# Gate sums divided out in the addition of delta, five held units, another order of the work

## The chip, the cores and the metric

The kernel runs on one core of a Trainium2 chip. The metric is device time in microseconds of that core, as the median of several runs. Engines in the profile: PE (TensorE, matrix products; PEld is its weight load), DVE (VectorE), ACT (ScalarE), POOL (GpSimd) and SP (SyncE, which here only issues DMAs). ScalarE issues DMAs too; the two issuers have a DMA ring each.

## The reference

```
# q, k, v, alpha: (4, 8, 768, 48) float32; state (48 x 48) for each of 4 x 8 heads
for t in range(768):
    state = alpha[t][:, None] * state + outer(k[t], v[t])
    y[t]  = q[t] @ state
x = y, heads side by side: (3072, 384)
logits = x @ w_gate                     # 8 experts
w = softmax over the 2 largest logits, 0 for the others
out = x + sum over e of w[e] * (x @ A[e]) @ B[e]      # rank 16 each
```

So a gated linear attention with a decay for every position and channel feeds a mixture of eight low-rank adapters.

## The kernel before

The 768 positions of a batch entry are cut into 6 chunks of 128; a chunk with all 8 heads is a *unit*, and there are 24 units, `u` = 0 to 23, of which 0, 6, 12 and 18 begin a batch entry ("batch 0" to "batch 3"). A unit is a tile of 128 positions x 384 columns. Each unit goes through the same steps, each a small function of the kernel:

- `ln` (ScalarE, mostly two units at once), `cum` (TensorE: sums of the logarithms to the chunk's end, in a PSUM bank), `exp` (ScalarE, twice: the decay and its inverse).
- `ka` and `kg` (GpSimd): `k` times one, `q` times the other, in bf16. Some units do both in one instruction of 128x768, those in `SPLIT` in two of 128x384.
- `tr` and `kq` (TensorE transposes, ScalarE copies), `at` (TensorE: the products of q and k, in the PSUM tile `at_t`), `msk` (VectorE: the causal mask, 128x1024, line 300).
- `vb` (GpSimd: `v` in bf16), `kv` (TensorE adds this chunk to the state in PSUM, `S_t`), `st` (VectorE scales the state by the decay, line 306). From unit to unit of a batch entry `st` and `kv` are a recurrence.
- `av` (TensorE: the unit's rows of y, in a bank), `ysb` (ScalarE copies them to `o_t[u]`), `xb` (GpSimd, bf16 copy, for the even units, `CAST`), `xt` and `xs` (TensorE transposes, ScalarE copies; in bf16 for `CAST` units, in float32 for the others).

The adapters work on *groups* of three units (the last two groups have two and one): `z` (TensorE: `x @ A` and the logits in one bank), `gm` (VectorE, the largest logits), `df`, `ge` and `gx` (difference to the largest, which are among the best two, exponential on ScalarE), `wu` (unnormalized weights), `dn` (their sum), `w` (reciprocal of the sum, and the weights times it, lines 416 and 419), `zw` (z times the weights, line 431), `zt` and `zs` (transposes, ScalarE copy). Then for each unit `dl` (TensorE: delta, in a bank, line 448), `o` (VectorE adds it to `o_t[u]`, line 455) and `out` (the store, issued by SyncE). Unit 23 alone is in `HOLD`: its `dl` is accumulated by TensorE onto its `av` bank, which is kept until then, and its `o` is a copy by ScalarE. The last group, which is unit 23, has its own short forms (lines 402 and 427).

PSUM has the tile `at_t` (two banks), the state `S_t`, and five banks `M_t` that `cum`, `tr`, `av`, `xt`, `z`, `zt` and `dl` share; the last number of an entry of the order says which of the five.

The order of everything is written out by hand in `ORDER`, one list for all engines: each engine takes its instructions in the order of the list, semaphores do the rest. `Sx.u.n` and `Ax.u.n` in it are loads issued by SyncE and by ScalarE: alpha (`a`), `q`, `k` and `v` of a batch entry come in one DMA each (48 rows of 48 numbers for each of 128 partitions), into two buffers of each that take turns. SyncE loads alpha and `q`, ScalarE loads `k` and `v`. A load of batch 2 or 3 waits until its buffer is free.

Of the kernel before, what the change touches and what calls it, by code (L numbers as in the profile page):

```python
# [9 lines left out]
ALU = mybir.AluOpType  # L10
# [3 lines left out]
F4 = mybir.dt.float32  # L14
# [4 lines left out]
DM = H * D  # L19
E = 8  # L20
R = 16
P = 128
# [8 lines left out]
GROUPS = [[0, 1, 2], [3, 4, 5], [6, 7, 8], [9, 10, 11], [12, 13, 14], [15, 16, 17], [18, 19, 20], [21, 22],  # L31
          [23]]
LNS = [[0], [1]] + [[u, u + 1] for u in range(2, NU, 2)]
CAST = set(range(0, NU, 2))
HOLD = {23}
SPLIT = {0, 1, 2, 3, 4, 5, 6, 7, 12, 13, 18, 19}
KEEP = dict(lg=2, ex=5, kg=6, kt=4, am=4, sb=3, vb=4, xs=9, xb=3, mx=3, xe=3, wu=3, dn=3, w=3, zw=3, zs=3)
NS = 6
MB = 5
ORDER = """  # L40
Sa.0.6 Aw.3.0 Sq.0.6 Aw.2.0 Sw.0.0 Ak.0.6 Sw.1.0 Sa.6.6 ln.0 Sq.6.6 ln.1 cum.0.0 cum.1.1 ln.4 exp.0 ln.2 exp.1
cum.2.2 Sa.12.6 ka.0 cum.5.3 Av.0.6 cum.3.4 exp.2 ka.1 exp.3 ka.2 kg.0 kg.1 tr.0.0 cum.4.1 kq.0 ka.3 tr.1.2 exp.5
at.0 kg.2 kq.1 msk.0 exp.4 kg.3 tr.2.4 cw.0 at.1 kg.4 msk.1 tr.3.0 Ak.6.6 kq.2 vb.0 kq.3 at.2 vb.1 kv.0 ka.4 av.0.3
st.1 ysb.0 msk.2 kv.1 vb.2 av.1.2 xb.0 tr.4.1 ysb.1 kg.5 st.2 at.3 xt.0.4 msk.3 ln.8 av.2.0 ka.5 Sq.12.6 kv.2 ln.6
st.3 vb.5 tr.5.3 xs.0 vb.4 ysb.2 cum.6.2 kq.4 cum.7.4 vb.3 kq.5 xb.2 at.4 exp.6 kv.3 msk.4 xt.2.0 xt.1.1 exp.7 ka.6
cum.9.3 st.4 cum.8.2 Av.6.6 xs.2 at.5 ln.10 ka.7 kv.4 msk.5 xs.1 Sa.18.6 exp.8 z.0.4 av.3.0 kg.6 exp.9 gm.0 av.4.1
st.5 ysb.3 kg.7 tr.6.2 ge.0 ysb.4 df.0 gx.0 av.5.3 kq.6 wu.0 kg.8 xt.3.0 dn.0 ysb.5 w.0 tr.7.1 xs.3 zw.0 at.6 kq.7
xt.5.2 msk.6 cum.11.3 xb.4 xs.5 zt.0.0 kg.9 xt.4.4 cum.10.1 xs.4 at.7 Ak.12.6 exp.10 tr.8.2 msk.7 z.1.4 zs.0 kq.8
vb.6 tr.9.1 gm.1 vb.7 exp.11 kv.6 at.8 kg.10 df.1 st.7 gx.1 av.6.0 msk.8 ln.12 av.7.2 kv.7 kq.9 cum.12.3 vb.8 st.8
ysb.6 dl.0.1 at.9 kg.11 ge.1 ysb.7 o.0 tr.10.0 ln.14 msk.9 av.8.2 kq.10 dl.2.1 kv.8 ysb.8 vb.9 dl.1.0 o.2 Sq.18.6  # L50
at.10 exp.12 vb.11 wu.1 cum.13.2 st.9 xt.7.1 xb.8 exp.13 dn.1 o.1 kv.9 xb.6 w.1 tr.11.3 Av.12.6 vb.10 xs.7 zw.1
cum.14.0 kq.11 ka.12 xt.8.2 msk.10 xt.6.1 zt.1.4 xs.8 cum.15.3 xs.6 zs.1 av.9.2 ka.13 exp.14 st.10 dl.3.1 z.2.4 o.3
ysb.9 kg.12 at.11 ln.16 gm.2 kv.10 msk.11 dl.4.0 kg.14 exp.15 tr.12.2 xt.9.1 kq.12 df.2 av.10.3 st.11 xs.9 cum.16.2
ge.2 o.4 gx.2 ysb.10 at.12 kg.13 wu.2 exp.16 tr.14.1 msk.12 dl.5.0 xb.10 kq.14 tr.13.3 kg.15 av.11.2 dn.2 o.5 kq.13
cum.17.1 w.2 Ak.18.6 xt.10.0 ysb.11 at.13 zw.2 xs.10 xt.11.3 msk.13 vb.12 tr.15.2 xs.11 vb.13 kv.12 exp.17 z.3.0
kg.16 st.13 at.14 ln.18 gm.3 av.13.4 msk.14 zt.2.3 kq.15 kv.13 cum.18.1 kg.17 zs.2 ysb.13 av.12.2 df.3 ge.3 st.14
at.15 ysb.12 tr.16.3 msk.15 exp.18 dl.7.4 vb.14 gx.3 tr.17.2 kq.16 wu.3 vb.15 o.7 kv.14 ln.20 vb.16 av.14.1 dn.3
st.15 xb.12 at.16 ysb.14 w.3 cum.19.3 vb.17 msk.16 kq.17 av.15.4 xb.14 Av.18.6 out.2 xt.13.1 exp.19 ka.18 out.7
kv.15 zw.3 xt.14.2 xs.13 at.17 st.16 xs.14 ka.19 xt.12.3 ysb.15 msk.17 zt.3.0 dl.6.1 xs.12 cum.20.2 ln.22 z.4.4
kg.18 o.6 zs.3 dl.8.3 exp.20 kv.16 gm.4 kg.19 tr.18.0 o.8 xt.15.1 kq.18 df.4 st.17 out.8 kg.20 dl.9.2 cum.21.3 xs.15  # L60
out.3 o.9 dl.10.0 gx.4 at.18 exp.21 out.5 o.10 tr.19.1 ge.4 msk.18 out.10 cum.22.2 kq.19 kg.21 av.17.0 out.6 exp.22
dl.11.3 av.16.1 wu.4 o.11 at.19 ysb.17 out.0 dn.4 tr.20.2 msk.19 ysb.16 out.9 vb.18 tr.21.3 kq.20 out.11 xb.16 kv.18
out.4 xt.17.0 kq.21 vb.19 w.4 st.19 at.20 out.1 vb.20 xs.17 xt.16.1 zw.4 cum.23.2 kg.22 xs.16 kv.19 msk.20 exp.23
z.5.3 st.20 at.21 kg.23 gm.5 av.18.0 tr.22.4 msk.21 ysb.18 kv.20 kq.22 av.20.1 ge.5 vb.21 df.5 at.22 st.21 gx.5
ysb.20 av.19.2 vb.22 wu.5 msk.22 zt.4.0 xb.18 ysb.19 kv.21 vb.23 tr.23.4 zs.4 dn.5 xb.20 dl.14.1 st.22 xt.19.2 kq.23
w.5 kv.22 xs.19 o.14 at.23 zw.5 xt.18.0 out.14 xt.20.4 msk.23 av.22.2 xs.18 xs.20 dl.12.1 z.6.3 ysb.22 o.12 xb.22
av.21.0 zt.5.4 gm.6 ysb.21 xt.22.2 dl.13.1 st.23 zs.5 xt.21.0 xs.22 df.6 ge.6 o.13 gx.6 dl.15.4 dl.17.2 xs.21 wu.6
o.15 av.23.1 z.7.0 dn.6 o.17 out.15 ysb.23 dl.16.4 out.13 gm.7 xt.23.2 w.6 out.17 df.7 ge.7 zw.6 gx.7 xs.23 wu.7
o.16 z.8.3 zt.6.2 gm.8 dn.7 out.16 zs.6 df.8 w.7 gx.8 out.12 dl.19.4 wu.8 dl.18.2 zw.7 o.18 zt.7.0 o.19 zs.7 dl.20.2
out.18 dl.21.0 w.8 o.20 dl.22.4 out.19 zw.8 out.20 o.21 zt.8.2 o.22 zs.8 out.21 dl.23 out.22 o.23 out.23  # L70
"""


# [6 lines left out]
def _bc(src: bass.AP, rep: int) -> bass.AP:  # L80
    aps = [list(x) for x in src.ap]
    return bass.AP(tensor=src.tensor, offset=src.offset, ap=aps + [[0, rep]])
# [9 lines left out]
def kernel(  # L92
# [11 lines left out]
    nc = tc.nc  # L104
# [11 lines left out]
    o_t = [big.tile([P, DM], F4, name=f"o_t{u}") for u in range(NU)]  # L116
# [21 lines left out]
    def act_copy(*args):  # L138
        recent[:] = [nc.scalar.copy(*args)]  # L139
# [56 lines left out]
    ex = ring("ex", [P, 2, DM + 2 * NP], F4)  # L196
# [7 lines left out]
    xe = ring("xe", [P, 3, E], F4)  # L204
    wut = ring("wu", [P, 3, E], F4)
    dnt = ring("dn", [P, 3], F4)
    wt = ring("w", [P, 3, E], F4)
    zwt = ring("zw", [P, 3, E, R], F2)
    zst = ring("zs", [P, 3 * HP], F4)
    W = consts.tile([P, NF, NZ], F2, name="W")  # L210
# [14 lines left out]
    def bank(s, i):  # L225
        return M_t[slot[s, i]]
# [112 lines left out]
                    start=(c == 0 and h == 0), stop=(h == H - 1 and u not in HOLD), skip_group_check=True)  # L339

    def ysb(u):
        act_copy(o_t[u], bank("av", u)[:, 0:DM])

    def xb(u):
        nc.gpsimd.tensor_copy(out=xbt[u % KEEP["xb"]], in_=o_t[u])  # L345

    def xt(u):
        if u in CAST:
            t, x, idn = bank("xt", u).bitcast(F2), xbt[u % KEEP["xb"]], ident
        else:  # L350
            t, x, idn = bank("xt", u), o_t[u], ident4
        x = x.rearrange("p (f i) -> p i f", i=NF)
        for i in range(NF):
            nc.tensor.transpose(t[:, i * P:(i + 1) * P], x[:, i, :], idn[:, :])  # L354

    def xs(u):
        t, y = bank("xt", u), xst[u % KEEP["xs"]].rearrange("p i t -> p (i t)")
        if u in CAST:
            act_copy(y.bitcast(F4), t[:, 0:DM // 2])
        else:  # L360
            act_copy(y, t[:, 0:DM])
# [5 lines left out]
    def scratch(g, i):  # L367
        n = len(GROUPS[g])
        lo = 3 * NZ + 3 * E * i
        return bank("z", g)[:, lo:lo + n * E].rearrange("p (n e) -> p n e", n=n)  # L370
# [28 lines left out]
    def wu(g):  # L399
        n = len(GROUPS[g])  # L400
        if n == 1:
            nc.vector.scalar_tensor_tensor(
                out=wut[g % KEEP["wu"]][:, 0, :], in0=zv(g)[:, 0, E * R:NZ], scalar=mx[g % KEEP["mx"]][:, 0, 1:2],
                in1=xe[g % KEEP["xe"]][:, 0, :], op0=ALU.is_ge, op1=ALU.mult, accum_out=dnt[g % KEEP["dn"]][:, 0:1])
            return
        nc.vector.tensor_tensor(out=scratch(g, 1), in0=scratch(g, 1),
                                in1=xe[g % KEEP["xe"]][:, 0:n, :], op=ALU.mult)

    def dn(g):
        n = len(GROUPS[g])  # L410
        nc.vector.tensor_reduce(out=dnt[g % KEEP["dn"]][:, 0:n], in_=scratch(g, 1),
                                op=ALU.add, axis=AX.X)

    def w(g):
        n = len(GROUPS[g])
        nc.vector.reciprocal(out=dnt[g % KEEP["dn"]][:, 0:n], in_=dnt[g % KEEP["dn"]][:, 0:n])
        if n == 1:
            return
        nc.vector.tensor_tensor(out=wt[g % KEEP["w"]][:, 0:n, :], in0=scratch(g, 1),
                                in1=_bc(dnt[g % KEEP["dn"]][:, 0:n], E), op=ALU.mult)  # L420

    def zw(g):
        n = len(GROUPS[g])
        zo = zwt[g % KEEP["zw"]][:, 0:n].rearrange("p n e r -> p (n e) r")
        z3 = zv(g)[:, :, 0:E * R].rearrange("p n (e r) -> p n e r", e=E)
        if n == 1:
            nc.vector.scalar_tensor_tensor(
                out=zo, in0=z3[:, 0], scalar=dnt[g % KEEP["dn"]][:, 0:1], in1=_bc(wut[g % KEEP["wu"]][:, 0, :], R),
                op0=ALU.mult, op1=ALU.mult)
        else:  # L430
            nc.vector.tensor_tensor(out=zwt[g % KEEP["zw"]][:, 0:n], in0=z3, in1=_bc(wt[g % KEEP["w"]][:, 0:n, :], R),  # L431
                                    op=ALU.mult)

    def zt(g):
        t = bank("zt", g).bitcast(F2)
# [15 lines left out]
    def o(u):  # L451
        if u in HOLD:
            act_copy(o_t[u], bank("av", u)[:, 0:DM])
        else:
            nc.vector.tensor_tensor(out=o_t[u], in0=bank("dl", u)[:, 0:DM], in1=o_t[u], op=ALU.add)  # L455

    def store(u):
        b, c = _place(u)
# [50 lines left out]
```

## Time and profile before

| | |
|---|---|
| median of 3 runs | 96.92 us (95.02 to 97.39) |
| the profiled execution | 94.6 us; span from first to last instruction 92.6 us; clock 0.971 |
| busy, share of the span | PE 68.6 us (74%), DVE 62.7 (68%), ACT 64.7 (70%), POOL 62.6 (68%) |
| moved | 24.17 MB, mean 261 GB/s: read 19.28 MB, written 4.72 MB |
| chain that ended last | DMA 33%, DVE 26%, ACT 16%, PE 11%, issue 5% |

A share of busy time is a mean over parts of the span with different limits, so it does not tell what a change is worth; for that one looks where each part of the span waits. In the slices of the page each digit is the busy share of a fortieth of the span in tenths. In the table of groups a row gives line, engine, operation, output and input, shapes and count, then the busy time and the mean duration of one in ns, then the idle time ahead of these instructions and what ended it. A timeline row gives start, duration and instruction.

### The profile page before, as it was taken

What the parts mean: (1) busy time and instruction counts of PE and PEld (TensorE: products, weight loads), DVE (VectorE), ACT (ScalarE), POOL (GpSimd) and SP (SyncE); (2) the same over time, 40 slices, a digit from 0 to 9 for tenths busy, and PEclk for the clock granted to TensorE, in tenths of its full rate; (3) what the DMA queues carried; (4) which work ended last, traced back from release to release, by engine and by line L of the source; (5) the groups of instructions that cost most, each with busy time, mean ns of one, the idle gap of its engine ahead of it and who ended that gap; (6) DMA issues with size and microseconds to landing.
All of it is one profiled execution on the core that took longest, in us unless ns stands there. A gap on an engine that the chain in (4) does not pass through costs nothing.

```text
span 92.6 us, 2795 instructions
## 1 busy us (share of the span) xinstructions
PE 68.6 (74%) x1088; PEld 54.0 (58%) x1088; DVE 62.7 (68%) x165; ACT 64.7 (70%) x164; POOL 62.6 (68%) x82
## 2 busy tenths in 40 slices
PE   0003080888899799959999998999999989994520
PEld 0002050756787697846787886887787878861100
DVE  5000000055956768887999999799999999999920
ACT  5004891695299998869999976999999666744120
POOL 6000087999795899997879999978999994200000
PEclk9999999999999999999999999999999999999855
DMA  1999999999999899999979999999996920216682
GB/s 25 282 309 317 315 317 315 303 314 304 317 312 298 233 309 311 281 303 304 302 229 316 311 281 305 307 306 251 289 383 227 342 94 7 85 52 250 258 295 84
DMA packets 29645, 24.17 MB, mean 261 GB/s; under 512 B 1856, under 2 KB 29632, under 8 KB 29632
## 3 DMA queue, kind: packets, MB, share of 16 engines
q1 hardware_dynamic: 16928, 14.35, 50.0%
q10 hardware_dynamic: 12704, 9.65, 36.6%
q8 instruction: 8, 0.13, 0.6%
q14 instruction: 5, 0.04, 0.2%
HBM read 19.28 MB, written 4.72 MB: 259 GB/s over the span
## 4 chain that ended last, share of the span: by engine, by line
DMA 33%; DVE 26%; ACT 16%; PE 11%; issue 5%; SPq 2%; ACTq 2%; POOL 1%; DVEq 0%
DMA a_t<-in_alpha_dram 18%; DMA kq_t<-in_q_dram 14%; DVE am L300 11%; ACT ex L136 5%; DVE o_t L455 5%; DVE sb L306 3%; ACT xs L139 3%; ACT o_t L139 3%; PE at_t L296 2%; PE M_t L283 2%; ACT lg L136 2%; ACT kt L139 2%; DVE zw L431 2%; PE M_t L448 2%; SPq L155 2%
## 5 line engine op out<-in xcount | busy, mean ns | idle before, releaser
L263 POOL TENSOR_TENSOR kgq<-kq_t,ex 128x384 bf16<-128x384 f32 (+1 forms) x36 | 45.0, 1275 | 12.4 <-ACT lg L136 9.8
L300 DVE TENSOR_TENSOR am<-at_t,mask 128x1024 bf16<-128x1024 f32 x24 | 29.3, 1220 | 20.5 <-PE at_t L296 20.4
L136 ACT ACTIVATE ex<-M_t 128x392 f32<-128x392 f32 (+1 forms) x48 | 21.6, 536 | 0.6 <-PE at_t L296 0.6
L283 PE MATMUL M_t<-ident,kgq 128*128 128x128 bf16 x192 | 17.0, 237 | 2.7 <-POOL kgq L263 2.6
L247 PE MATMUL M_t<-lg,suf 128*128 128x384 bf16 x24 | 8.6, 366 | 12.3 <-ACT lg L136 12.3
L139 ACT COPY kt<-M_t 128x512 f32<-128x512 f32 x24 | 14.6, 618 | 4.1 <-PE M_t L283 3.5
L139 ACT COPY o_t<-M_t 128x384 f32<-128x384 f32 x25 | 12.4, 521 | 5.5 <-PE M_t L337 4.7
L136 ACT ACTIVATE lg<-a_t 128x768 bf16<-128x768 f32 (+1 forms) x13 | 10.5, 824 | 8.0 <-DMA a_t<-in_alpha_dram 7.2
L283 PEld LDWEIGHTS <-kgq 128*128 128x128 bf16 x192 | 12.8, 105 | 4.6 <-POOL kgq L263 3.1
L455 DVE TENSOR_TENSOR o_t<-M_t,o_t 128x384 f32<-128x384 f32 x23 | 12.4, 550 | 1.1 <-PE M_t L448 1.1
L306 DVE TENSOR_TENSOR sb<-S_t,ex 128x384 bf16<-128x384 f32 x20 | 11.0, 549 | 1.2 <-PE S_t L320 1.2
L277 POOL CAST vb<-v_t 128x384 bf16<-128x384 f32 x24 | 11.6, 507 | 0.0
L296 PE MATMUL at_t<-kt 48*128 48x128 bf16 x192 | 10.2, 229 | 1.4 <-DVE am L300 1.0
L337 PE MATMUL M_t<-vb,am 128*128 128x48 bf16 x192 | 9.0, 186 | 0.0
L345 POOL CAST xb<-o_t 128x384 bf16<-128x384 f32 x12 | 6.0, 507 | 4.4 <-ACT o_t L139 4.3
L248 PEld LDWEIGHTS <-ident 128*128 128x128 bf16 x24 | 2.4, 101 | 11.2 <-issue 10.9
L296 PEld LDWEIGHTS <-kt 48*128 48x128 bf16 x192 | 6.2, 98 | 4.1 <-issue 1.9
L448 PE MATMUL M_t<-B_all,zs 128*128 128x384 bf16 x24 | 7.5, 334 | 1.0 <-ACT zs L139 0.8
L337 PEld LDWEIGHTS <-am 128*128 128x128 bf16 x192 | 7.3, 99 | 0.3
L354 PE MATMUL M_t<-ident,o_t 128*128 128x128 f32 x36 | 6.9, 302 | 0.2 <-DVE o_t L455 0.2
L320 PE MATMUL S_t<-vb,kgq 128*128 128x96 bf16 x80 | 7.0, 213 | 0.0
L330 PE MATMUL M_t<-sb,kt 128*128 128x96 bf16 x80 | 6.9, 209 | 0.1
(53 smaller groups left out, 101.0 us busy)
## 6 DMA issues: line engine op xcount, KB each, us to landing
out_dram<-o_t SPq DMA_DIRECT2D x24, 192.0 KB, 2.1
B_st<-in_moe_B_dram ACTq DMA_DIRECT2D x1, 192.0 KB, 2.7
W_st<-in_moe_A_dram SPq DMA_DIRECT2D x2, 96.0 KB, 9.4
a_t<-in_alpha_dram SPq DMA_DIRECT2D x4, 0.2 KB, 12.9
kq_t<-in_q_dram SPq DMA_DIRECT2D x4, 0.2 KB, 16.4
kq_t<-in_k_dram ACTq DMA_DIRECT2D x4, 0.2 KB, 8.1
v_t<-in_v_dram ACTq DMA_DIRECT2D x4, 0.2 KB, 8.1
G_st<-in_moe_w_gate_dram ACTq DMA_DIRECT2D x1, 12.0 KB, 4.1
```

What stands on the lines that cost most here:

```text
L136: recent[:] = [nc.scalar.activation(*args, **kw)]
L139: recent[:] = [nc.scalar.copy(*args)]
L247: nc.tensor.matmul(r[:, 0:DM], suf[:, :], t[:, :, 0:D], start=True, stop=True)
L263: nc.gpsimd.tensor_tensor(out=kgq[u % KEEP["kg"]][:, part, :, 0:D], in0=kq_t[b % 2].rearrange("p w (h c) d -> p w c h d", c=NCH)[:, part, ...
L277: nc.gpsimd.tensor_copy(out=vbt[u % KEEP["vb"]], in_=chunks(home("v", b))[:, c, :, 0:D])
L283: nc.tensor.transpose(t[:, w, p, :], pair(kgq[u % KEEP["kg"]][:, w], p), ident[:, :])
L296: nc.tensor.matmul(at_t[:, hh, p, :], kq[rows, 0, p, :], kq[rows, 1, p, :], start=True, stop=True)
L300: nc.vector.tensor_tensor(out=am[u % KEEP["am"]].rearrange("p a b t -> p (a b) t"), in0=at_t.rearrange("p a b t -> p (a b) t"), in1=_bc_mi ...
L306: nc.vector.tensor_tensor(out=sb[u % KEEP["sb"]].rearrange("p a b d -> p (a b) d"), in0=S_t.rearrange("p a b d -> p (a b) d"), in1=_bc(ex[ ...
L337: nc.tensor.matmul(y[:, h * D:(h + 1) * D], am[u % KEEP["am"]][:, hh, p, :], vbt[u % KEEP["vb"]][:, h, :], start=(c == 0 and h == 0), stop ...
L448: nc.tensor.matmul(bank("av" if hold else "dl", u)[:, 0:DM], zst[g % KEEP["zs"]].bitcast(F2)[:, j * P:(j + 1) * P], B_all[:, :], start=not ...
L455: nc.vector.tensor_tensor(out=o_t[u], in0=bank("dl", u)[:, 0:DM], in1=o_t[u], op=ALU.add)
```

## The change

- The weights are no longer divided by their sum. `wu` writes the unnormalized weights to SBUF, `zw` uses them, `w` is only the reciprocal, and `o` becomes one instruction that multiplies delta by the reciprocal (a scalar for each position) and adds `o_t`. `dn` has six buffers and not three.
- `HOLD` grows from {23} to {5, 11, 17, 21, 23}. For a held unit in a group of several, `zw` is a separate instruction that includes the reciprocal, since its delta is added by TensorE. `ysb` of a held unit writes the bf16 tile `xb` directly, so that held units are transposed in bf16 like those of `CAST`; `o` copies the sum from the bank.
- `ORDER` is another list, in which nearly every engine's instructions are permuted among units and banks. SyncE's nine loads stay in their order, ScalarE's loads stay in theirs, and stand elsewhere among its other instructions.

```diff
-HOLD = {23}
+HOLD = {17, 5, 21, 23, 11}
-KEEP = dict(... xs=9, xb=3, mx=3, xe=3, wu=3, dn=3, w=3, zw=3, zs=3)
+KEEP = dict(... xs=9, dn=6, xb=3, mx=3, xe=3, wu=3, w=3, zw=3, zs=3)
 ORDER = """
-Sa.0.6 Aw.3.0 Sq.0.6 Aw.2.0 Sw.0.0 Ak.0.6 Sw.1.0 Sa.6.6 ln.0 Sq.6.6 ln.1 cum.0.0 cum.1.1 ln.4 exp.0 ln.2 exp.1
-cum.2.2 Sa.12.6 ka.0 cum.5.3 Av.0.6 cum.3.4 exp.2 ka.1 exp.3 ka.2 kg.0 kg.1 tr.0.0 cum.4.1 kq.0 ka.3 tr.1.2 exp.5
-at.0 kg.2 kq.1 msk.0 exp.4 kg.3 tr.2.4 cw.0 at.1 kg.4 msk.1 tr.3.0 Ak.6.6 kq.2 vb.0 kq.3 at.2 vb.1 kv.0 ka.4 av.0.3
+Sa.0.6 Aw.3.0 Sq.0.6 Aw.2.0 Sw.0.0 Ak.0.6 Sw.1.0 Sa.6.6 ln.1 Sq.6.6 ln.0 cum.1.0 Av.0.6 cum.0.1 exp.1 exp.0 ln.2
+ka.1 ln.4 cum.2.2 ka.0 exp.2 cum.4.3 cum.3.4 exp.4 cum.5.0 ka.2 exp.3 kg.0 Sa.12.6 kg.2 tr.0.1 exp.5 kq.0 kg.1
+Ak.6.6 at.0 ka.3 msk.0 tr.1.2 tr.2.3 kq.1 kg.5 kq.2 at.1 cw.0 msk.1 vb.0 vb.1 av.0.4 kv.0 kg.3 ysb.0 st.1 at.2 msk.2
...
-av.21.0 zt.5.4 gm.6 ysb.21 xt.22.2 dl.13.1 st.23 zs.5 xt.21.0 xs.22 df.6 ge.6 o.13 gx.6 dl.15.4 dl.17.2 xs.21 wu.6
-o.15 av.23.1 z.7.0 dn.6 o.17 out.15 ysb.23 dl.16.4 out.13 gm.7 xt.23.2 w.6 out.17 df.7 ge.7 zw.6 gx.7 xs.23 wu.7
-o.16 z.8.3 zt.6.2 gm.8 dn.7 out.16 zs.6 df.8 w.7 gx.8 out.12 dl.19.4 wu.8 dl.18.2 zw.7 o.18 zt.7.0 o.19 zs.7 dl.20.2
-out.18 dl.21.0 w.8 o.20 dl.22.4 out.19 zw.8 out.20 o.21 zt.8.2 o.22 zs.8 out.21 dl.23 out.22 o.23 out.23
+xs.18 xt.20.1 o.17 at.23 o.16 xs.20 av.22.2 ysb.21 msk.23 out.16 z.6.3 ysb.22 kv.22 xb.22 gm.6 xt.21.1 xt.22.4 xs.21
+df.6 ge.6 dl.15.2 st.23 gx.6 xs.22 wu.6 z.7.1 o.15 av.23.4 dn.6 gm.7 out.15 w.6 ge.7 ysb.23 out.12 df.7 zw.6 gx.7
+out.17 xt.23.2 wu.7 zt.6.3 dn.7 xs.23 w.7 zs.6 z.8.2 zw.7 dl.18.3 gm.8 zt.7.1 df.8 o.18 zs.7 gx.8 dl.21 out.18 wu.8
+dl.22.1 dl.19.3 o.21 w.8 o.22 dl.20.0 out.21 zw.8 o.20 out.22 zt.8.1 zs.8 o.19 out.20 dl.23 out.19 o.23 out.23
 """
...
     def ysb(u):
-        act_copy(o_t[u], bank("av", u)[:, 0:DM])
+        act_copy(xbt[u % KEEP["xb"]] if u in HOLD else o_t[u], bank("av", u)[:, 0:DM])
...
     def xt(u):                      # and xs(u) likewise
-        if u in CAST:
+        if u in CAST | HOLD:
...
     def wu(g):
-        nc.vector.tensor_tensor(out=scratch(g, 1), in0=scratch(g, 1),
+        nc.vector.tensor_tensor(out=wut[g % KEEP["wu"]][:, 0:n, :], in0=scratch(g, 1),
                                 in1=xe[g % KEEP["xe"]][:, 0:n, :], op=ALU.mult)
...
     def w(g):
-        nc.vector.reciprocal(out=dnt[g % KEEP["dn"]][:, 0:n], in_=dnt[g % KEEP["dn"]][:, 0:n])
-        if n == 1:
-            return
-        nc.vector.tensor_tensor(out=wt[g % KEEP["w"]][:, 0:n, :], in0=scratch(g, 1),
-                                in1=_bc(dnt[g % KEEP["dn"]][:, 0:n], E), op=ALU.mult)
+        r = dnt[g % KEEP["dn"]][:, 0:n]
+        nc.vector.reciprocal(out=r, in_=r)
 
     def zw(g):
...
+        free = [j for j, u in enumerate(GROUPS[g]) if u not in HOLD and n > 1]
+        for j in set(range(n)) - set(free):
             nc.vector.scalar_tensor_tensor(
+                out=zo[:, j], in0=z3[:, j], scalar=dnt[g % KEEP["dn"]][:, j:j + 1], in1=_bc(wu[:, j, :], R),
                 op0=ALU.mult, op1=ALU.mult)
+        if free:
+            part = slice(free[0], free[-1] + 1)
+            nc.vector.tensor_tensor(out=zo[:, part], in0=z3[:, part], in1=_bc(wu[:, part, :], R), op=ALU.mult)
...
     def o(u):
         if u in HOLD:
             act_copy(o_t[u], bank("av", u)[:, 0:DM])
         else:
-            nc.vector.tensor_tensor(out=o_t[u], in0=bank("dl", u)[:, 0:DM], in1=o_t[u], op=ALU.add)
+            g, j = gof[u]
+            y, d = o_t[u], bank("dl", u)[:, 0:DM]
+            if len(GROUPS[g]) == 1:
+                nc.vector.tensor_tensor(out=y, in0=d, in1=y, op=ALU.add)
+            else:
+                nc.vector.scalar_tensor_tensor(out=y, in0=d, scalar=dnt[g % KEEP["dn"]][:, j:j + 1], in1=y,
+                                               op0=ALU.mult, op1=ALU.add)
```

## The prediction

> **What bounds the kernel now.** I read the slices of the whole span first, then the table of stretches, then the rows of the engines in the stretch that ends last.
>
> ```profile
> PE   0003080888899799959999998999999989994520
> DVE  5000000055956768887999999799999999999920
> ACT  5004891695299998869999976999999666744120
> POOL 6000087999795899997879999978999994200000
> DMA  1999999999999899999979999999996920216682
> ```
>
> Each digit is 2.3 us. The DMA row is full from 2.3 to about 69 us, and all four engines are above eight tenths from about 30 us on: up to there the loads set the pace and no engine is far behind. From slice 31 (71.8 us) the DMA row falls to 0 to 2, POOL and ACT empty, and DVE alone stays at 9 up to 88 us. So the end has another limit than the middle. GpSimd's rows show where one hands over to the other:
>
> ```profile
> 64.29 5.53 POOL L263 TENSOR_TENSOR kgq<-kq_t,ex 128x384 bf16<-128x384 f32 x4 [0.36 <-DMA kq_t<-in_q_dram]
> 69.76 0.50 POOL L277 CAST vb<-v_t 128x384 bf16<-128x384 f32 x1
> ```
>
> The last `q` load lets go at 64.2 us (issued 47.24, 17.0 us to landing), the last `v` load at 69.6 (issued 60.71, 8.9 to landing). The stretches after it (us; then busy PE, PEld, DVE, ACT, POOL, clock, DMA share, GB/s):
>
> ```profile
> 66.00:72.00 6.00, 5.90 (x107) 4.61 (x105) 5.94 (x14) 5.67 (x14) 6.00 (x8) 1.00 0.87 298
> 72.00:78.00 6.00, 5.60 (x108) 4.80 (x106) 5.93 (x17) 4.20 (x11) 5.42 (x7) 1.00 0.46 169
> 78.00:84.00 6.00, 5.21 (x82) 3.98 (x76) 5.90 (x24) 3.44 (x11) 0.51 (x1) 1.00 0.26 96
> ```
>
> VectorE works 17.77 of 18 us, so in this stretch time is VectorE's instructions added up. The last mask of the first unit of batch 3 (`msk.18`) starts at 67.42, the last gate product (`zw.8`) ends at 87.60; 1.77 us later `o.23` is done, then comes its store. What follows is counted between those two instructions, 20.18 us.
>
> **Prices.** Groups, mean ns of one at the end of "busy":
>
> ```profile
> L455 DVE TENSOR_TENSOR o_t<-M_t,o_t 128x384 f32<-128x384 f32 x23 | 12.4, 550 | 1.1 <-PE M_t L448 1.1
> L431 DVE TENSOR_TENSOR zw<-M_t,w 128x384 bf16<-128x384 f32 x7 | 3.9, 552 | 0.1
> L431 DVE TENSOR_TENSOR zw<-M_t,w 128x256 bf16<-128x256 f32 x1 | 0.4, 419 | 0.0
> L427 DVE SCALAR_TENSOR_TENSOR zw<-M_t,dn,wu 128x128 bf16<-128x128 f32 x1 | 0.3, 342 | 0.0
> ```
>
> Queued instructions overlap a little, so a removed one is worth the distance between starts:
>
> ```profile
> 70.40 0.17 DVE L416 RECIPROCAL dn<-dn 128x3 f32<-128x3 f32 x1
> 70.60 0.18 DVE L419 TENSOR_TENSOR w<-M_t,dn 128x24 f32<-128x24 f32 x1
> 70.70 0.56 DVE L306 TENSOR_TENSOR sb<-S_t,ex 128x384 bf16<-128x384 f32 x1
> ...
> 85.42 0.42 DVE L431 TENSOR_TENSOR zw<-M_t,w 128x256 bf16<-128x256 f32 x1
> 85.75 1.01 DVE L455 TENSOR_TENSOR o_t<-M_t,o_t 128x384 f32<-128x384 f32 x2
> 86.68 0.15 DVE L416 RECIPROCAL dn<-dn 128x1 f32<-128x1 f32 x1
> 86.78 0.56 DVE L455 TENSOR_TENSOR o_t<-M_t,o_t 128x384 f32<-128x384 f32 x1
> 87.26 0.34 DVE L427 SCALAR_TENSOR_TENSOR zw<-M_t,dn,wu 128x128 bf16<-128x128 f32 x1
> 87.52 1.01 DVE L455 TENSOR_TENSOR o_t<-M_t,o_t 128x384 f32<-128x384 f32 x2
> ```
>
> - A `w` product: reciprocal to next start is 0.30 us with it (70.40 to 70.70) and 0.10 without (86.68 to 86.78), so 0.20.
> - An addition of 128x384: 0.47 (two take 1.01, one lasts 0.55).
> - `zw` of 128x384 also 0.47, of 128x256 0.33 (85.42 to 85.75); a straight line gives 0.19 for 128x128.
> - SCALAR_TENSOR_TENSOR of 128x128: 0.26 (87.26 to 87.52), 0.07 over that line.
>
> The new addition, a 128x384 SCALAR_TENSOR_TENSOR, is not in this trace. From below it costs what the plain one does, +0; from above the same ratio, 0.26/0.19 of 0.47, +0.17. The one-unit `wu` (L402, 128x8) lasts 225 ns against 172 to 175 for plain two-input ones of 8 or 16 columns, and 128x128 shows an excess of about the same size, so it is a fixed amount: I take +0.07.
>
> **The change part by part.**
>
> 1. *Division moved into the addition.* VectorE loses eight `w` products: -8 x 0.20 = -1.60. Nineteen additions become SCALAR_TENSOR_TENSOR: 19 x 0.07 = +1.33 (0 to +3.2). Writing `wu` to SBUF and not to PSUM changes the same two small instructions per group; rows of 24 columns are 175 to 186 ns whatever they read, so I take 0, bounds -0.2 and +0.2 in all. The six `dn` buffers only let an addition wait longer.
> 2. *Five held units.* Units 5, 11, 17 and 21 join 23: delta is accumulated in their `av` bank. VectorE loses four additions (-4 x 0.47 = -1.88) and gets `zw` in two pieces in four groups (0.26+0.33-0.47 three times, 0.26+0.19-0.33 once: +0.48). ScalarE gets four copies (0.48 each, +1.9) and saves on five `xs`, whose narrow copy is 355 ns and not 528 (-0.9). In the stretch that counts, the copies of 11, 17 and 21 have ScalarE's free 0.33, 1.80 and 2.56 us of the three stretches to lie in; the copy of unit 5 falls before 60 us, where ScalarE is at nine tenths, and may push 0.3 us there, which the wait for `q` at 64.2 hides. TensorE: 15 transposes go from 302 to 221 ns and their weight loads from 200 to 104; they lie under VectorE. What is new is that a held bank is missing from the five `M_t` banks from `av` to `o`; I take 0 and price it as a rival.
> 3. *The order.* SyncE's nine loads keep their order. ScalarE's loads stand up to six instructions earlier: `v` of batch 0 moves ahead of the first two exponentials, `k` of batch 1 goes from behind the weight casts (issued at 20.10) to behind `kq.0` (17.08 to 17.67 now). The later ones move by two to four. In ScalarE's queue only issue rows of 0.7 us are concerned, and the loads hide behind earlier ones in the ring: `v` of batch 0 is behind `k`, which lands at 11.9; `k` of batch 1 starts when `v` lands, at 19.25. The gain is at most the 0.9 us from 19.25 to 20.10 for ScalarE's ring; taken from SyncE's `q` it would be a loss. I take 0 at the end, since the 64.2 of the last `q` follows from bytes. GpSimd does the same 72 casts and products; `kg.5` and two `vb` move ahead of `kg.3` (1.0 + 0.95), which makes unit 3 later by 2 us, inside the 16.4 us between two `q` landings. On SyncE the stores are reordered: the first one now asks for `o.5`, done at 53.3 us even in the old order; SyncE comes to its stores only when it has issued its last load (55.4 us).
>
> One rule speaks against part 3. The Trainium skill, "DMA: Bandwidth & Descriptors", section "Queues, rings and completion order", says that each DMA engine takes packets in turn from the queues that have work, so an earlier load on one queue slows the other and moves no byte sooner. This trace agrees in that it holds about 310 GB/s with both rings filled and 302 to 321 while ScalarE's ring is empty from 19.3 to 21.3 us. By the rule the earlier `k` load would cost SyncE's next `q` about half of its lead, later given back; the sum stays as it is.
>
> **The sum for the end.** VectorE's order is read from the two order lists. Between `msk.18` and `zw.8` the new list has nine additions where the old has ten (-0.47); `zw.4` with its small instructions is done before `msk.18` (-0.47-0.55); `w.5` to `w.7` are gone (-0.60); two groups are split (+0.24); nine additions are the dearer form (9 x 0.07 = +0.63). Sum -1.22: 20.18 becomes 18.96. `msk.18` itself can start when `at.18` is done, 67.08 and not 67.42, and VectorE, 0.45 us lighter before it (-1.67 in all, -1.22 of it behind), gets there: -0.34. Together -1.56, so `zw.8` ends at 86.0. The other chain allows it: `msk.23` would start at 79.2 (five masks, six additions, four state products, group 5: 12.1 us), later than now (78.46), but only 6.6 us of work follows it up to `zw.8`.
>
> The profiled execution took 94.6 us (span 92.6 and 2.0 around it); the sum gives 93.0, a ratio of 0.984. The median of the runs shown is 96.92, 2.5% above that execution: 96.92 x 0.984 = 95.3. With the bounds of the new addition (nine times 0 to 0.17) the end moves by -2.2 to -0.7; with 1 us for the order either way, 93.6 to 97.3 is this case's own range. Differences under 2% can hardly be told from none in this kernel.
>
> **Rivals.**
>
> - *Held banks stop TensorE (slower).* TensorE's queue is in order: when a matmul waits for a bank, `at`, `kv` and `tr` of the next units wait behind it, and VectorE's masks for these. Unit 17 holds its bank over 21 uses of the others, unit 21 over 17, and a `z` bank is held too, from `z.5` (72.1) to `zw.5` (78.5): three banks are left. From 69 to 78.5 that is 9.5 x 3 / 20 = 1.4 us for a use; a `tr` use takes 0.61+0.59 plus handover, a `cum` use 0.5+0.9. It is tight, which speaks for it; that the waits view has only 0.4 us of TensorE waiting for `o` now speaks against. If ten of the 38 uses wait for half a use, 0.5 us each, the price is 5 us, less the 1.6 gained: 94.6+3.4, at the median 100.4. It decides from 3.5 us of such waits on.
> - *The early part gets shorter as well (faster).* The dips to 130 to 230 GB/s around 30, 47 and 63 us cost about 3 us of full rate. If the loads' turns close half of that, the last `q` lands 1.5 us sooner, and the end gains 3.1: 93.7. Against it: these dips stand at the starts of SyncE's loads, which do not move.
> - *Nothing (same).* Latency, not VectorE, sets the end: `av.23` waits for `xs.22` and `z.7` ahead of it, and what VectorE saves becomes idle time. Then 96.9.
>
> **How the numbers follow.** The sum's case 0.60, of which about half lies past 2%; the rival faster 0.14; nothing 0.04; slower 0.22. Faster 0.46, within 2% 0.29, slower 0.25 (part of the sum's tail). The range takes in the faster rival with the low bound, 92.8, and the lower part of the slow one, 98.8.
>
> **What would show it.** VectorE's sum of busy time down by about 2 us; additions near 0.61 us each; `msk.18` near 67, `msk.23` near 79; no TensorE wait for `o` over 1 us. A `msk.18` later than 68.5, or VectorE idle for more than 1.5 us behind it, makes the prediction wrong.

## The result, and the profile after

The changed kernel took 104.03 us (median; 103.54 to 104.75), the kernel before, run beside it, 95.97: a ratio of 1.096 (95% interval 1.085 to 1.107). The ratio, here and below, leaves out the slower ones of a kernel's executions (two of the four of the kernel before, near 97 us), so it is not the quotient of the medians. The changed kernel is slower by 8 to 9 us, where 95.3 us and a gain were forecast. The profiled execution has a span of 102.0 us, 9.4 more than before.

The slices of the whole span (one digit 2.55 us), kernel after:

```profile
PE   0004182979969978999993007999999999996830
DVE  5000000476248829999898000968998999999850
ACT  5004996273799988998970019769999756765320
POOL 6000389999469599999994007952999998310000
PEclk9999999999999999999999855569999999999655
DMA  2999999999998999999994998963920082223473
```

Up to slice 20 (counted from 0) this looks like the kernel before. ScalarE falls to 0 in slice 21 (from 53.6 us), and in slices 22 and 23 (56.1 to 61.2 us) all four engines are at 0 or 1 while the DMA row stands at 9: the core has stopped, and the loads go on. The clock row (PEclk, the granted TensorE clock in tenths) is 8, 5, 5, 5, 6 in slices 22 to 26, where the kernel before shows nines up to its last three slices. Near the end the DMA row drops to 0 for two slices and comes back with the late stores.

ScalarE's timeline (start, duration, what; in brackets the idle time before and its releaser) shows who stopped first, kernel after:

```profile
52.48 0.60 ACT L139 COPY kt<-M_t 128x512 f32<-128x512 f32 x1
60.08 0.02 ACT L155 MOVE_SHAPE kq_t<-in_k_dram  x1 [6.99 <-issue]
60.13 0.70 ACTq L155 DMA_DIRECT2D kq_t<-in_k_dram  x1
```

ScalarE is done at 53.08 and stands 6.99 us in front of the issue of one load, `k` of batch 3 (`Ak.18`). The kernel before issued it at 52.77 with no wait before it:

```profile
52.72 0.02 ACT L155 MOVE_SHAPE kq_t<-in_k_dram  x1
52.77 0.70 ACTq L155 DMA_DIRECT2D kq_t<-in_k_dram  x1
```

The waits of the kernel after (engine, line, releaser; us in total, times, longest):

```profile
DVE sb L305 <- PE S_t L319: 11.6, 4, 7.8
POOL kgq L262 <- ACT ex L136: 9.3, 3, 7.2
PE M_t L434 <- ACT ex L136: 7.3, 1, 7.3
ACT kq_t L155 <- issue: 7.0, 1, 7.0
```

The other three rows are what was queued behind that load on ScalarE: its next `exp`, and with it GpSimd's products (7.2 us), TensorE (7.3) and VectorE's state products (7.8). "issue" for 7.0 us says only that the profile shows no releaser. Two numbers point to it: the last `q` load was issued at 46.68 and landed 13.3 us later, at 59.98, and ScalarE went on at 60.08:

```profile
kq_t<-in_q_dram SPq DMA_DIRECT2D x1, 0.2 KB, 13.3
46.68 7.44 SPq L155 DMA_DIRECT2D kq_t<-in_q_dram  x1
```

The waits in the two built programs say why a `k` load should wait for a `q` load that it shares nothing with. Each DMA signals its end on one of eight semaphores. The framework deals these in turn, in the order in which its scheduler expects the DMAs to run, which is not the order of the list: in both lists the stores stand behind `Ak.18`, and some are dealt ahead of it all the same. Before the issue of a DMA the program waits until the DMA eight places earlier has landed. In the kernel before only one store (`out.2`) is dealt ahead of `Ak.18`, which is DMA number 20; number 12, the alpha load of batch 2, is long done. In the kernel after six stores (`out.5`, `1`, `0`, `2`, `4`, `3`) are dealt ahead of it. It is number 25, and number 17 is the last `q` load. The `v` load behind it is number 28 and shares with number 20, the store `out.1`.

The 9.4 us of the span come apart as follows, each a difference of two times in the traces: `Ak.18` could have gone at 53.09 and not 52.72, +0.4; the hole, +7.0; from its issue to `msk.18` 17.26 (60.13 to 77.39) and not 14.65, +2.6; from `msk.18` to the end of `zw.8` -0.3; the rest -0.3.

The stretches inside that path (us; busy PE, PEld, DVE, ACT, POOL with counts, granted clock, DMA share, GB/s), after:

```profile
50.00:60.00 10.00, 4.34 (x85) 3.81 (x83) 5.66 (x15) 3.02 (x8) 4.64 (x4) 0.89 0.92 265
60.00:70.00 10.00, 8.13 (x107) 6.66 (x107) 5.28 (x10) 7.36 (x19) 5.84 (x7) 0.60 0.80 253
77.39:97.30 19.91, 17.80 (x265) 12.83 (x264) 19.12 (x55) 12.55 (x35) 10.42 (x14) 0.95 0.30 111
```

From 60 to 70 us TensorE is busy for 8.1 of 10 us at a clock of 0.60. The third row is the stretch that the prediction counted: 19.91 us with VectorE at 19.12.

### The profile page after: what moved, and what is told of

Same layout as the page of the kernel before. It is cut to its first block, busy times and chain, and to the rows that moved or that the text cites. A ratio compares the mean times of both kernels' runs of the same rounds, so it can differ in the third digit from the quotient of the medians.

```text
span 102.0 us, 2797 instructions
## 1 busy us (share of the span) xinstructions
PE 71.9 (70%) x1088; PEld 56.0 (55%) x1088; DVE 61.9 (61%) x157; ACT 66.0 (65%) x168; POOL 62.7 (61%) x82
## 4 chain that ended last, share of the span: by engine, by line
PE 28%; POOL 21%; issue 18%; DMA 13%; DVE 9%; ACT 6%; SPq 1%; ACTq 1%; POOLq 0%; DVEq 0%
POOL kgq L262 15%; DMA kq_t<-in_q_dram 13%; PE M_t L282 6%; PE at_t L295 4%; POOL vb L276 4%; PE M_t L445 3%; DVE o_t L457 3%; DVE am L299 2%; PE M_t L353 2%; PE M_t L336 2%; PE M_t L329 2%; POOL xb L344 2%; PE S_t L314 2%; PE S_t L319 2%; ACT ex L136 2%
## 5 line engine op out<-in xcount | busy, mean ns | idle before, releaser
L136 ACT ACTIVATE ex<-M_t 128x392 f32<-128x392 f32 (+1 forms) x48 | 20.8, 514 | 3.7 <-PE M_t L250 2.0
L282 PEld LDWEIGHTS <-kgq 128*128 128x128 bf16 x192 | 13.6, 110 | 3.5 <-POOL kgq L262 2.0
L139 ACT COPY o_t<-M_t 128x384 f32<-128x384 f32 x24 | 11.9, 500 | 5.0 <-PE M_t L336 3.9
L457 DVE SCALAR_TENSOR_TENSOR o_t<-M_t,dn,o_t 128x384 f32<-128x384 f32 x19 | 11.3, 608 | 2.3 <-ACT ex L136 1.9
L336 PE MATMUL M_t<-vb,am 128*128 128x48 bf16 x192 | 9.5, 190 | 0.3 <-DVE am L299 0.2
L445 PE MATMUL M_t<-B_all,zs 128*128 128x384 bf16 x24 | 8.3, 389 | 1.3 <-ACT zs L139 1.2
L434 PE MATMUL M_t<-ident,zw 128*128 128x128 bf16 x24 | 3.1, 233 | 7.9 <-ACT ex L136 7.3
L319 PEld LDWEIGHTS <-kgq 128*128 128x128 bf16 x80 | 6.1, 106 | 2.3 <-issue 1.0
```

The source lines that it names most:

```text
L136: recent[:] = [nc.scalar.activation(*args, **kw)]
L282: nc.tensor.transpose(t[:, w, p, :], pair(kgq[u % KEEP["kg"]][:, w], p), ident[:, :])
L319: nc.tensor.matmul(S[:, p].rearrange("p b d -> p (b d)"), pair(kgq[u % KEEP["kg"]][:, 0], p), pair(vbt[u % KEEP["vb"]], p), start=(c == 0 ...
L336: nc.tensor.matmul(y[:, h * D:(h + 1) * D], am[u % KEEP["am"]][:, hh, p, :], vbt[u % KEEP["vb"]][:, h, :], start=(c == 0 and h == 0), stop ...
L445: nc.tensor.matmul(bank("av" if hold else "dl", u)[:, 0:DM], zst[g % KEEP["zs"]].bitcast(F2)[:, j * P:(j + 1) * P], B_all[:, :], start=not ...
L457: nc.vector.scalar_tensor_tensor(out=y, in0=d, scalar=dnt[g % KEEP["dn"]][:, j:j + 1], in1=y, op0=ALU.mult, op1=ALU.add)
```

## The experiments

**The stores later, nothing else.** The six first stores go behind `out.6` in the list of the changed kernel, so that `Ak.18` is DMA number 19 (eight before: `k` of batch 1) and `Av.18` number 22 (`v` of batch 1):

```diff
-... msk.15 z.3.1 Av.18.6 out.5 exp.18 av.14.3 out.1 kv.14 xb.12 out.0 gm.3 ysb.14 at.16 out.2 ge.3 ...
-... kg.18 out.4 zt.3.1 kv.16 out.3 zs.3 xt.15.3 gm.4 ln.22 out.6 kg.19 ...
+... msk.15 z.3.1 Av.18.6 exp.18 av.14.3 kv.14 xb.12 gm.3 ysb.14 at.16 ge.3 ...
+... kg.18 zt.3.1 kv.16 zs.3 xt.15.3 gm.4 ln.22 out.6 out.5 out.1 out.0 out.2 out.4 out.3 kg.19 ...
```

> The changed kernel, with SyncE's stores in another order: the store of unit 6 comes first, so that the six stores of units 5, 1, 0, 2, 4 and 3 are dealt their semaphores after ScalarE's load of k for batch 3. That load then shares its semaphore with the k load of batch 1 and no longer with SyncE's last q load. Theory A (the 7.0 us hole at 53 to 60 us is ScalarE waiting for a semaphore shared with the last q load): the load of k is issued near 53 us, no ScalarE gap above 1 us there, and the time falls by about 7 us, 104.0 to 96 to 97.5. Rival B (held PSUM banks stop TensorE): the hole stays, 103 to 105. Rival C (the new order is itself slower, and the hole only hides it): 99 to 102.

Measured: 93.62 us against 95.55, ratio 0.977 (0.958 to 0.996). Span 90.7. Timeline of ScalarE's queue, and of VectorE, of this kernel:

```profile
51.01 0.70 ACTq L155 DMA_DIRECT2D kq_t<-in_k_dram  x1
66.45 1.22 DVE L299 TENSOR_TENSOR am<-at_t,mask 128x1024 bf16<-128x1024 f32 x1 [0.24 <-PE at_t L295]
78.67 1.22 DVE L299 TENSOR_TENSOR am<-at_t,mask 128x1024 bf16<-128x1024 f32 x1
85.70 0.34 DVE L424 SCALAR_TENSOR_TENSOR zw<-M_t,dn,wu 128x128 bf16<-128x128 f32 x1
```

The `k` load goes at 51.01, there is no hole, `msk.18` starts at 66.45 (77.39 in the kernel after), `msk.23` at 78.67, and `zw.8` ends at 86.04. The place of six stores is worth 10 us. Units held in PSUM and division are the same in both, so neither made the kernel slow.

**One DMA more.** The store order of the changed kernel stays; a second load of the 12 KB gate weights, which changes nothing in the result, is put ahead of `Av.12`. It shifts the numbers by one: `Ak.18` is now 26 and shares with that small load.

```diff
-wu.1 vb.10 st.9 at.9 Sq.18.6 Av.12.6 kq.10 ...
+wu.1 vb.10 st.9 at.9 Sq.18.6 Aw.2.0 Av.12.6 kq.10 ...
```

> The changed kernel with one DMA of 12 KB more (the gate weights, loaded a second time by ScalarE ahead of v of batch 2), and nothing else changed. It moves the load of k for batch 3 from the semaphore of the last q load to that of this small load. Theory A: 104.0 falls by 5 to 7 us, though one DMA is added (the v load of batch 3 now shares with the second store, which may hold it for some 2 us). Rivals B and C: 104 to 105, as one more DMA can only cost.

Measured: 101.27 us, ratio 1.064 (1.054 to 1.075). The hole at `k` is gone (issued at 52.55), as expected, but only 2.8 us came back. The waits of this kernel name what I had priced at 2 us:

```profile
ACT v_t L155 <- DMA out_dram<-o_t: 5.5, 1, 5.5
```

`Av.18`, now number 29, shares with the store `out.1` (21), which SyncE issues only behind its last load; it went at 65.51, 7.9 us later than in the kernel with the stores later. So one added DMA removes one hole and leaves the other: TensorE waits 5.9 us here for an exponential of ScalarE's that is queued behind the `v` load. In the kernel after, the second one is covered by the first: its `v` load, at 68.71, has no idle time before it.

**The kernel before, made to share.** The opposite way: in the list of the kernel before the stores of units 2, 0, 1, 3, 4 and 5 come first (taken from their later places, not printed here), so that five of them are dealt ahead of `Ak.18`. The small extra load, in the first of two kernels only, moves `Ak.18` from number 24 (sharing with `k` of batch 2) to 25 (sharing with the last `q`):

```diff
-... tr.11.3 Av.12.6 ...
+... tr.11.3 Aw.2.0 Av.12.6 ...                 # in the first kernel only
...
-... xb.14 Av.18.6 out.2 xt.13.1 ...            # in both
+... xb.14 Av.18.6 out.2 out.0 out.1 out.3 out.4 out.5 xt.13.1 ...
```

> The kernel before, with the stores of units 2, 0, 1, 3, 4, 5 first and the same extra load of 12 KB, which together put the load of k for batch 3 on the semaphore of the last q load. Theory A: ScalarE stops for 6 to 8 us near 53 us here too, and the time rises from 96 to 102 to 105. Rival B or C: 96 to 98, since order, banks and arithmetic are those of the kernel before.

> The same as the run before it without the extra 12 KB load: the stores of units 2, 0, 1, 3, 4, 5 first, and the load of k for batch 3 on the semaphore of the k load of batch 2. Theory A: no hole at 53 us, 96 to 99 (the v load of batch 3 now shares with the first store, up to 3 us late). Rival B or C: the same as the run before it.

Measured: sharing with the last `q` 105.44 us, ratio 1.110 (1.096 to 1.124); control 100.49, 1.055 (1.042 to 1.069). The waits view of the first one now names the releaser; the second row is the control's:

```profile
ACT kq_t L154 <- DMA kq_t<-in_q_dram: 7.7, 1, 7.7
ACT v_t L154 <- DMA out_dram<-o_t: 3.4, 1, 3.4
```

7.7 us for the last `q`, in the code and the order of the kernel before: between these two kernels, 5 us apart, only a load of 12 KB differs. The control missed its expectation of 96 to 99. Its `Av.18` (27) shares with its first store (19): ScalarE stood 3.4 us in front of it, the load went at 64.54, 3.8 us later than before, and `msk.18` started at 72.47, 5.05 later. I had asked whether the data of `v` can come later. What counts is ScalarE, which stands in front of the issue with its next exponential behind it, and TensorE waits 4.1 us for that one. How the 5.05 divide between the wait and the lower clock behind it (last section) no run shows.

**Parts one at a time.** All with the first stores placed where they hold up no load, so that the three parts of the change can be read. "Without division" puts the eight `w` products, the plain additions and the gate product in one piece back; "without held units" lets VectorE add units 5, 11, 17 and 21, whose banks are still kept until then; "order alone" does both; "division alone" is the kernel before with part 1 only.

```diff
 # without division
+        if n > 1:
+            nc.vector.tensor_tensor(out=wt[g % KEEP["w"]][:, 0:n, :], in0=scratch(g, 1), in1=_bc(r, E), op=ALU.mult)
...
 # without held units (the bank stays with the unit)
-HOLD = {17, 5, 21, 23, 11}
+HOLD = {23}
+KEPT = {17, 5, 21, 11}
...
-            y, d = o_t[u], bank("dl", u)[:, 0:DM]
+            y, d = o_t[u], bank("av" if u in KEPT else "dl", u)[:, 0:DM]
```

> The kernel before with the division moved into the addition and nothing else (order, held unit and store order as before). By the prediction's prices VectorE loses eight products (8 x 0.20 = 1.6 us) and gets 23 dearer additions (23 x 0.07 = 1.6 us): the same time as before within 1%. Rival (fewer instructions on VectorE are a gain by themselves, the dearer addition is not seen): 1 to 2% faster.

> The changed kernel with the stores in the order of the first run, and the division back in its own product (eight products more, 19 plain additions, zw of a group in one piece). By the prices +1.6 - 1.3 - 0.5 on VectorE, and between the first mask of batch 3 and the last zw +0.6 - 0.6 - 0.2: within 0.5 us of the first run, 93 to 94. Rival (the division is where the gain is): as slow as before, 95.5.

> The changed kernel with the stores in the order of the first run, and the additions of units 5, 11, 17 and 21 back on VectorE (their banks still kept, their transposes in float32 again, zw in one piece). By the prices VectorE gets 4 x 0.54 - 0.48 = +1.7 us in all, three of the four additions behind the first mask of batch 3 (+1.4): 95 against 93.6. Rival (held units are worth nothing, or cost by ScalarE's copies): 93.6 or less.

> The first run's kernel beside the next two on one chip. By its first measurement 0.977 of the kernel before, between 0.96 and 0.99.

> The changed kernel with the stores later and the division back in its own product, beside the run before it on one chip. By the prices within 0.5 us of it; if the dearer additions weigh more than the products behind the last q load, up to 0.5 us faster, else the same.

> The order alone: the changed kernel's order with the stores later, the division back in its own product, and units 5, 11, 17 and 21 added by VectorE. If held units are worth the 1.4 us of their additions in the end, this is about 1.4 us slower than the run before it, 95 to 95.6. If the order itself is the gain, it stays near 94.

> The changed kernel with its first stores later, once more, in five rounds beside the same kernel with the division put back, to settle what the division is worth. From the prices of the prediction the division saves 8 x 0.20 on VectorE and costs 19 x 0.06 in the additions, 0.5 us in all, about half of it behind the first mask of batch 3: ratio to the kernel before 0.978 to 0.985, and 0.003 to 0.006 below that of the kernel with the division put back. Rival: the division is worth nothing, since VectorE's removed products lie where it waits for TensorE anyway: then both ratios are within 0.002 of each other.

> The changed kernel with its first stores later and the gate sums divided out in the weights as before (eight w products back, additions plain). If the division is worth 0.3 to 0.5 us, its ratio is 0.982 to 0.990; if the division is worth nothing, the same as that of the kernel with the division moved, 0.978 to 0.985; if the earlier 0.970 stands, the division costs time, and the ratio is below that of its neighbour by about 0.007.

| kernel (stores later unless said) | ratio to before, interval | `msk.18` starts, us | from there to the end of `zw.8`, us |
|---|---|---|---|
| before, as it is | 1 | 67.42 | 20.18 |
| division alone (list of before) | 0.993 (0.989 to 0.997) | 68.44 | 20.10 |
| order alone | 0.996 (0.991 to 1.002) | 69.35 | 20.32 |
| order and division, no held units | 0.983 (0.975 to 0.990) | 68.12 | 20.67 |
| order and held units, no division | 0.970 (0.964 to 0.975), 0.990 (0.981 to 0.998), 0.984 (0.977 to 0.992) | 68.30, 68.02, 68.48 | 19.61, 19.62, 19.61 |
| all three | 0.977 (0.958 to 0.996), 0.982 (0.975 to 0.990), 0.992 (0.988 to 0.996) | 66.45, 66.68, 68.00 | 19.59, 19.60, 19.59 |

What follows. The stretch is steady to 0.01 us where one kernel was profiled three times, and it answers both questions. Its time can be split by what stands on VectorE, each instruction counted from its start to the next start (the last to its end):

| us of VectorE from `msk.18` to the end of `zw.8` | before | new order, held units, no division | all three |
|---|---|---|---|
| small instructions of group 4 | 0.55 | 0 | 0 |
| small instructions of groups 5 to 8, with `w` | 3.60 | 4.40 | 3.80 |
| additions | 4.84 (ten) | 4.48 (nine) | 4.82 (nine) |
| gate products `zw` | 2.08 | 1.62 | 1.86 |
| masks and state products | 9.11 | 9.11 | 9.11 |
| sum | 20.18 | 19.61 | 19.59 |

Division is worth nothing in the stretch (20.10 against 20.18 alone, 19.59 against 19.61 with held units), and the last two columns say why: three `w` products less save 0.60, the dearer form of nine additions costs 0.34, and two gate products in two pieces 0.24. Held units shorten the stretch by 0.71 us without division (20.32 to 19.61) and by 1.08 with it (20.67 to 19.59), where 1.4 had been expected. Nearly all of it is two additions fewer, eleven to nine: 0.83 (5.31 to 4.48) and 1.02 us (5.84 to 4.82). Both kernels without held units have the lower clock of the last slices inside the stretch (granted 0.97 and 0.91 over it, against 1.00 in those with held units); it can have a part only in the rest. What the clock can do there the kernel after shows, with 0.95 and the code of the last row: its stretch took 19.91, 0.32 longer, all in one wait of an addition for TensorE's delta:

```profile
95.83 0.16 DVE L416 RECIPROCAL dn<-dn 128x1 f32<-128x1 f32 x1
96.43 0.62 DVE L457 SCALAR_TENSOR_TENSOR o_t<-M_t,dn,o_t 128x384 f32<-128x384 f32 x1 [0.44 <-PE M_t L445]
```

The two starts are 0.60 apart here and 0.28 with the stores later.

The ratio of one kernel moves by 1.5 to 2% from one measurement to the next (on one chip the four runs of the first one lie between 92.63 and 94.77 us), so the whole-kernel ratios can't tell 0.3 us; in the last two pairs, each on one chip, division came out 0.7% faster once and 0.8% slower once. The last pair meets neither of its expectations: the ratio with division is not 0.003 to 0.006 lower, and the two are not within 0.002 of each other. "Worth nothing" rests on the stretch, and not for the reason given with it: the removed products do save their time. "Order alone" is no change that can be told from the kernel before. All three with the stores later stand at 0.977, 0.982 and 0.992: a version that beats the kernel before by 1 to 2%.

## Why the prediction was wrong, point by point

**The step that failed** is the third of "The change part by part", and in it the words "On SyncE the stores are reordered [...] SyncE comes to its stores only when it has issued its last load" and "I take 0 at the end, since the 64.2 of the last `q` follows from bytes". I followed each queue by itself. The stores do not delay SyncE's loads, that was right; what six stores dealt ahead of `Ak.18` do is move ScalarE's next load onto the semaphore of the last `q`. The prediction named the exponentials that ScalarE's loads pass, but priced no wait of a load and so never asked what is queued behind one. Measured, this was 7.0 us of hole in the profile, and 10.4 us between two kernels that differ in the place of six stores (104.03 and 93.62). The price of part 3 was 0, with "1 us for the order either way". The prediction's own test, "`msk.18` later than 68.5", shows it: 77.39.

**The rival on the slower side** had the right sign (100.4 us; 104.03 measured) for the wrong reason. Held banks were to stop TensorE. With the stores later the same banks are held in the same order and the kernel is faster than before; of TensorE's waits in its profile only this one can be for an `o`:

```profile
PE M_t L445 <- ACT o_t L139: 0.2, 1, 0.2
```

The kernels without held units keep the same banks, so they say nothing on this.

**The sum of parts 1 and 2** had the right sign, and by the kernel with the stores later its end (86.0) was met at 86.04 and 86.28, but at 87.59 in the third profile. The agreement is in part luck: `msk.18` was to start at 67.08 and started at 66.45, 66.68 and 68.00, and the stretch, forecast to shrink from 20.18 to 18.96, took 19.59. Half of the 1.22 us is missing. Most of its terms were right. The counts are: nine additions in the stretch and not ten. The added form, from the groups of the kernel with the stores later (line, form, count, busy, mean ns):

```profile
L457 DVE SCALAR_TENSOR_TENSOR o_t<-M_t,dn,o_t 128x384 f32<-128x384 f32 x19 | 11.3, 609 | 2.0 <-ACT ex L136 1.9
```

609 ns, 59 more than the 550 of the plain addition; I took 70. In the table above nine of them cost 0.34 more than plain ones, and the sum had 0.63. Group 4's small instructions (0.55), the split gate products (0.24) and the 0.20 for a `w` product came out as priced. The last one shows in the same list with the product (kernel "order and held units, no division") and without it ("all three"):

```profile
77.10 0.16 DVE L417 RECIPROCAL dn<-dn 128x3 f32<-128x3 f32 x1
77.30 0.18 DVE L419 TENSOR_TENSOR w<-M_t,dn 128x24 f32<-128x24 f32 x1
77.40 0.55 DVE L306 TENSOR_TENSOR sb<-S_t,ex 128x384 bf16<-128x384 f32 x1
...
75.44 0.17 DVE L416 RECIPROCAL dn<-dn 128x3 f32<-128x3 f32 x1
75.52 0.53 DVE L305 TENSOR_TENSOR sb<-S_t,ex 128x384 bf16<-128x384 f32 x1
```

Reciprocal to the next large instruction is 0.30 us with the product and 0.08 without. What the sum left out is the new order's own cost: it took the small instructions of groups 5 to 8 at their old price, and in the new list, with the `w` products still there, they take 4.40 us and not 3.60. Of the 0.80, 0.18 is a wait for TensorE behind the last reciprocal (0.10 us to the next start before, 0.28 now). The rest is mostly this: where a large instruction stood behind a small one, the next small one, which needs its result, now often stands there. The largest part, 0.33, lies at the gate maxima (`gm`, MAX8), before and with the stores later:

```profile
80.05 0.31 DVE L381 MAX8 mx<-M_t 128x8 f32<-128x8 f32 x3
80.28 0.54 DVE L306 TENSOR_TENSOR sb<-S_t,ex 128x384 bf16<-128x384 f32 x1
...
71.49 0.31 DVE L380 MAX8 mx<-M_t 128x8 f32<-128x8 f32 x3
71.83 0.19 DVE L387 TENSOR_TENSOR M_t<-M_t,mx 128x24 f32<-128x24 f32 x1
```

Three maxima cost 0.23 us there and 0.34 here. In group 7 a whole chain stands together in the kernel with the stores later:

```profile
82.69 0.16 DVE L405 TENSOR_TENSOR wu<-M_t,xe 128x16 f32<-128x16 f32 x1
82.88 0.17 DVE L410 TENSOR_REDUCE dn<-wu 128x2 f32<-128x16 f32 x1
83.09 0.17 DVE L416 RECIPROCAL dn<-dn 128x2 f32<-128x2 f32 x1
83.29 0.35 DVE L424 SCALAR_TENSOR_TENSOR zw<-M_t,dn,wu 128x128 bf16<-128x128 f32 x1
```

Each waits for the result of the one before, and the starts are 0.19, 0.21 and 0.20 us apart. Together: 0.80 for the order less 0.18 that the additions cost less than the sum had is the 0.63 by which the stretch is longer than forecast, to 0.01.

**A reading of the slices** was off as well: TensorE's row stands at 8 and 9 up to 83 us in the kernel before, so VectorE was not alone at 9. The sum still holds, since VectorE is busy for 19.13 of the 19.59 us, but a slower TensorE shows at once, as the wait of 0.44 us above does.

**VectorE's busy time** was to fall by about 2 us (parts 1 and 2 add up to -1.67); it fell from 62.7 to 61.9 in the kernel after and to 61.2 with the stores later.

**The rival "early part shorter"** came in part. With the stores later the last `q` load landed at 62.3, 62.9 and 64.0 us in three profiles, against 64.2 before: 1.9, 1.4 and 0.3 us sooner, where the rival said 1.5, and `Ak.18` went at 51.01 in the first and at 52.47 in the third, against 52.77. Most of the difference between the 66.45 and the 68.00 of `msk.18` is there by then, and no run shows what decides it. In the kernel after the last `q` landed 4.3 us sooner, at 59.98, while `k` was not yet issued, and nothing came of it.

**"Nothing"** was the forecast's tail and is what part 3 alone gives once the stores are out of the way (0.996).

**The rule on queues** weighed in the prediction (the Trainium skill, "DMA: Bandwidth & Descriptors", section "Queues, rings and completion order": engines take packets in turn from the queues that have work) speaks of transfers already issued. It was not what decided: in the seven microseconds of the hole the kernel after moved 246 GB/s, and the load that everything waited for had not been issued.

## What to carry to other kernels

When a list of instructions is reordered, number the DMAs in the order in which the program deals their completion semaphores, which need not be the order of the list, and write beside each which DMA holds the same one before it: moving stores, which seem free, can hang a load of another queue on a late transfer, and everything behind that load on its engine stops with it. Price a small instruction by what stands behind it, in the new order and not in the old: here it costs 0.08 to 0.10 us where the next one does not need its result and about 0.2 where it does, and a list that brings dependent ones together lost about the 0.6 us that three removed products saved. Where the same kernel's ratio moves by 1 to 2% between measurements, compare the distance between two marks of the trace, which here repeated to 0.01 us.

## What the runs showed of the hardware that I had not expected

From the stop on TensorE ran slow. The clock row has 8, 5, 5, 5, 6 from the middle of the hole of the kernel after, 0.60 over the ten microseconds from 60 to 70. The three other kernels in which ScalarE stood in front of a late load show a like dip at their own places, here the kernel before made to share, and below it the clock row of its control:

```profile
PEclk9999999999999999999999655589999999999975
62.00:72.00 10.00, 9.09 (x138) 8.00 (x139) 6.02 (x16) 7.41 (x19) 4.66 (x8) 0.73 0.71 213
PEclk9999999997599999999999999965599999999755
```

Cut into stretches of 1 us, the four agree: TensorE stops at 54.4, 54.5, 61.3 and 62.2 us (kernel after, the kernel before made to share, one DMA more, the control), the granted clock falls from 1.00 to 0.50 between 1.9 and 3.3 us after that, still inside the stop, and it is back at 1.00 at 68.0, 67.5, 70.4 and 70.9, after TensorE has worked again for 3 to 6 us. In the kernel after these are six microseconds of full work at a clock of 0.50, from 62 to 68. None of the kernels with the stores later has a dip before its last four slices, where the kernel before has one too. The control has one dip more, at 23 to 27 us, with no late load ahead of it; TensorE was busy there for 2.3 of the 4 us from 20 to 24, and for 3.0 in the kernel before, which has no dip. So a full stop is not the only thing that goes with one.

From `Ak.18` to `msk.18` the kernel after took 17.26 us, and 15.44 and 15.53 in two profiles of the same code with the stores later: 1.8 us more, of which the slow clock is the likely cause. That the idle time causes the dip, and the dip the 1.8 us, is argued from their coming together; no run held the one and changed the other.
